# Attention scores in shared columns: 18 steps a segment instead of 20, with a new opening and a new order

## The chip, the cores and the metric

The kernel runs on one core of a Trainium2 chip. The core's engines work side by side, each with its own queue of instructions: the tensor engine (PE, with its weight loads shown as PEld), VectorE (DVE), ScalarE (ACT), GpSimd (POOL) and SyncE (SP), which issues most of the DMA transfers. The metric is the device time of one execution in microseconds (us); the shorter, the better. Before the change the median of three runs is 550.27 us (549.77 to 551.29).

## The reference

Two layers of attention and two of a gated feed-forward block (FFN) alternate over 2048 tokens of width 512. Attention has 32 heads of 16 channels and works on four segments of 512 tokens, one after the other. Inside a segment it is causal softmax attention; beside it each segment reads a memory that earlier segments have summed up.

```python
def _A_ref(x, wq, wk, wv, wo, beta):
    ...
    for s in range(N):                      # N = 4 segments of L = 512
        qs, ks, vs = (q[:, :, s].copy(), k[:, :, s].copy(), v[:, :, s].copy())
        logits = jnp.einsum('bhqd,bhkd->bhqk', qs, ks) * scale + mask
        p = _softmax(logits, axis=-1)
        a_dot = jnp.einsum('bhqk,bhkd->bhqd', p, vs)
        pq = phi(qs)
        a_mem = jnp.einsum('bhld,bhde->bhle', pq, M) / (jnp.einsum('bhld,bhd->bhl', pq, z)[..., None] + 1e-06)
        outs.append(g * a_mem + (1.0 - g) * a_dot)
        pk = phi(ks)
        M = M + jnp.einsum('bhld,bhle->bhde', pk, vs)
        z = z + jnp.einsum('bhld->bhd', pk)
    ...
def _B_ref(x, w_gate, w_up, w_down):
    return _gelu(x @ w_gate) * (x @ w_up) @ w_down
x = x + _A_ref(_layernorm(x), ...)
x = x + _B_ref(_layernorm(x), ...)
x = x + _A_ref(_layernorm(x), ...)
x = x + _B_ref(_layernorm(x), ...)
```

## The kernel before, in words

The work is cut into eight segments `k` (NK): four of the first pair of layers and four of the second. Attention (class `Att`) and FFN (class `Ffn`) of a segment go through the same engines as those of its neighbours, mixed so that PE always has something to issue.

**Scores.** The heads of a segment lie in four blocks `b` of eight; in a block, four even heads (`par` 0) and four odd ones (`par` 1) are worked on together. Keys stand on partitions, queries in columns. A *step* (`steps_of`, L154) fills 512 columns for each of four heads: two PSUM tiles `st` of 128 x 1024. The four heads sit in four groups of 32 rows of the PE array ("row tiles", `tile_position=(32 * j, 0)`, L974): even heads read keys from `kf`, rows 32j to 32j + 16, odd heads from `kB`, a copy of the keys in which the even heads' rows are zero, so that 32 rows can be used. Causality leaves of the 4 key tiles `ki` 512, 384, 256 and 128 columns, 1280 for a head, and two and a half steps hold 1280 columns: five steps a block and parity pair, 20 a segment. ScalarE takes the exponential of each `st` into `pt` (L1005, 128 x 1024), and GpSimd sets the part above the diagonal of a diagonal tile to zero (`affine_select`, L992). `PT_STEPS` = 5 sets of `pt` buffers go round.

**Flushes.** `flush_item` (L1013) multiplies a block's finished `pt` with V (L1039): four pieces, one for each key tile, each as four matmuls side by side in groups of 32 columns of the array ("column tiles"). `vaug` holds, for each head, 16 channels of V and a constant, which gives the softmax's sum. DVE then transposes, divides and transposes back (L1063 to L1078), and POOL adds the memory's part (L1082).

**Everything else on PE** (projections, the memory's products, gate, up, down, the output product) runs through `product` (L524 to L527): four matmuls in column tiles, 512 columns in a group of four.

**Order.** The whole order is written at build time. `Clocks` keeps an estimated time for each engine; work items carry a due time (`DUE`, `DUE_STEP`, `BIAS` and the constants from L42 to L70) and a condition; the loop at L1396 takes the next step of scores when its PSUM is free, else a step of the open item, else a ready item, and, where nothing is ready, a filler product with the tile `warm`. Every engine's queue then has this fixed order, and each instruction waits for the semaphores of what it reads.

**Opening** (L1272 to L1328, outside the planner). 17 filler matmuls run while the first 512 tokens arrive. DVE takes the statistics of four tiles (`bn_stats`, `bn_aggr`), POOL turns them into scales (`first_scale`), DVE normalises (`normed`), PE transposes (`first_turn`), and the first K and Q follow. `gate` (two DVE operations on the memory's gate) stands between the second and the third normalised tile. For segment 0, `kB` of block 0 is made by DVE, that of the other blocks by four DMA copies (`odd_heads`, L692).

**Copies on SP's queue.** Four copies of 64 KB a segment fill `kB`; transposing DMAs turn normalised rows (`xnT`), the memory's output (`amT`) and `phik`; weights and outputs go through the same queue. Three sets of Q, K, `kB` and `vaug` go round (`SETS`).

Of the kernel before, what the change touches and what calls it, by code (L numbers as in the profile page):

```python
# [18 lines left out]
P = 128  # L19
# [17 lines left out]
STEPS = 20  # L37
BY_PE = {("xnTf", 0)}
M_BANKS = 4
PT_STEPS = 5  # L40
SETS = 3
# [3 lines left out]
N3 = 0.0  # L45
GELU_TILES = 2
QK_DUE = 0.696
E_Q = -0.446
E_K = 1.142

FLUSH_WAIT = 5.222
PIECE_SLACK = 3.936
URGENT, SOON, NORMAL = -9.238, -1.856, 0.0
EXP_SLACK, E_SLACK, PHI_SLACK, GELU_SLACK = -0.955, 5.474, 2.934, 5.676
ACT_EVICT, FIRST_EVICT = 4.1, -0.181
XN_BUFS = 4
XN_KEPT = 1
XNA1_PE = 0
NORM_HALVES = 8
RAWS = [7, 7, 9, 6, 8, 8, 10]  # L60
FLUSH_FIRST = -1.999
SECOND_EVICT = 0.375
E_BUFS = 2
KB_SLACK = 8.054
HALF_STEPS = 2
LAST_FIRST = 8
MARGIN = 1.7
PHI_MARGIN = 1.7
KB_MARGIN = 1.5
MEM_SLACK = -2.323  # L70


DUE = {"wo": 0.456, "gate": 1.084, "up": 1.34, "down": 1.726, "upd": 0.124, "mem": 0.239, "v": -0.013}
DUE_STEP = {"gate": 0.0103, "up": 0.0229, "down": 0.0643}
BIAS = {
    **{("qk", *k): d for k, d in {
# [4 lines left out]
    }.items()},  # L81
    **{("mem", *k): d for k, d in {
        (0,): 0.334, (0, 0): -0.435, (1,): -0.094, (1, 0): 0.056, (2,): 0.396, (3,): 0.144, (3, 0): 0.04,
        (4,): -0.223, (4, 0): -0.207, (5,): -0.239, (5, 0): -0.057, (6,): -0.101, (6, 0): 0.015, (7,):
        -0.117, (7, 0): 0.048
    }.items()},
    **{("down", *k): d for k, d in {
# [4 lines left out]
    }.items()},  # L92
    **{("upd", *k): d for k, d in {
        (0,): -0.507, (0, 0): 0.188, (1,): 1.18, (1, 0): 0.412, (2,): -0.142, (2, 0): 0.095, (3,): 1.042,
        (3, 0): -0.249, (4,): -0.368, (4, 0): 0.137, (5,): 0.506, (5, 0): -0.155, (6,): 0.023, (6, 0):
        0.323, (7,): 0.107
    }.items()},
    **{("v", *k): d for k, d in {
# [4 lines left out]
    }.items()},  # L103
    **{("wo", *k): d for k, d in {
# [3 lines left out]
    }.items()},  # L108
    **{("gate", *k): d for k, d in {
# [5 lines left out]
    }.items()},  # L115
    **{("up", *k): d for k, d in {
# [4 lines left out]
    }.items()},  # L121
    **{("num", *k): d for k, d in {
# [5 lines left out]
    }.items()},  # L128
    **{("ek", *k): d for k, d in {
# [14 lines left out]

def bias(kind, k, i=None):
    return BIAS.get((kind, k), 0) + BIAS.get((kind, k, i), 0)


HALF = L // 2
SPLIT = {NK - 1}  # L150
EARLY = 1


def steps_of(k):  # L154


# [76 lines left out]
class Clocks:  # L233
# [57 lines left out]
    def made(self):  # L291

        return self.pe + 0.15
# [1169 lines left out]
```

## Time and profile before

| | |
|---|---|
| median of three runs | 550.27 us (549.77 to 551.29) |
| profiled execution, whole | 550.23 us |
| its span from the first to the last instruction | 548.5 us |
| PE busy | 542.0 us, 99% |
| ScalarE busy | 442.3 us, 81% |
| VectorE busy | 418.5 us, 76% |
| GpSimd busy | 270.9 us, 49% |
| granted PE clock | 1.000 |

In the profile's rows, "L527 PE MATMUL m<-xnT,wu_sb 128*32 128x512" is line 527 on PE, writing tile `m` from `xnT` and `wu_sb`, 128 rows by 32 columns of the array, 512 columns streamed; "x40" counts instructions, and the figures behind the bar are busy time, mean duration of one, and idle time before with what ended it. In a timeline the first two columns are start and length in us. In rows of waits the figures are the total, the count and the longest. In the chain of waits they are start and length along the chain.

### The profile page before, as it was taken

The numbers are of one execution on the slowest core, as the hardware profiler recorded it, in microseconds if no ns is written. First come the engines' busy times: TensorE is split into PE (matmuls) and PEld (weight loads), VectorE is DVE, ScalarE is ACT, GpSimd is POOL, SyncE is SP. The second block draws the span as 40 slices with busy tenths as digits, with TensorE's granted clock in tenths as the row PEclk, the third lists the DMA queues.
The fourth block names the chain that finished last, engine by engine and source line by source line (L and its number), as shares of the span: only waits on it lengthen the run. The fifth ranks groups of instructions, "written<-read, shape, count | busy, mean of one in ns | idle before, by whom it ended". The sixth has DMA issues, their size and how long they took to land.

```text
span 548.5 us, 25412 instructions
## 1 busy us (share of the span) xinstructions
PE 542.0 (99%) x11372; PEld 263.5 (48%) x11372; DVE 418.5 (76%) x790; ACT 442.3 (81%) x530; POOL 270.9 (49%) x541
## 2 busy tenths in 40 slices
PE   8999999999999999999999999999999999999997
PEld 4333444444454444444444444444454445545984
DVE  5878895899869798678777798587985789776162
ACT  5899999997999779987799879998889777872500
POOL 4686553576635664627542466257662472322000
PEclk9999999999999999999999999999999999999999
DMA  7357535140633125200230123111431005102201
GB/s 231 47 125 223 116 42 146 22 51 14 73 56 43 11 41 80 50 13 12 41 60 12 23 31 61 32 20 43 50 72 22 3 12 89 23 3 51 32 5 41
DMA packets 69885, 29.11 MB, mean 53 GB/s; under 512 B 59280, under 2 KB 69264, under 8 KB 69776
## 3 DMA queue, kind: packets, MB, share of 16 engines
q1 hardware_dynamic: 69632, 27.48, 26.1%
q8 instruction: 89, 1.46, 1.2%
q14 instruction: 20, 0.16, 0.1%
q10 hardware_dynamic: 144, 0.01, 0.0%
HBM read 9.71 MB, written 2.10 MB: 22 GB/s over the span
## 4 chain that ended last, share of the span: by engine, by line
PE 89%; DVE 5%; ACT 2%; issue 1%; DMA 1%; POOL 0%; DVEq 0%; ACTq 0%
PE m L527 71%; PE st L974 10%; PE m L1039 6%; ACT pt L1005 2%; DVE x_sb L1137 1%; PE m L425 1%; DVE st L550 1%; DMA xnT<-xn 1%; PE m L887 1%; DVE byq L1063 0%; DVE e L790 0%; DVE phiq L772 0%; DVE xn L586 0%; DVE aT L1078 0%; DVE e L798 0%
## 5 line engine op out<-in xcount | busy, mean ns | idle before, releaser
L1005 ACT ACTIVATE pt<-st 128x1024 bf16<-128x1024 f32 x320 | 309.6, 1029 | 54.6 <-PE st L974 49.7
L992 POOL TENSOR_SCALAR_AFFINE_SELECT pt<-pt 128x512 bf16<-128x512 bf16 (+2 forms) x416 | 197.6, 493 | 189.2 <-ACT pt L1005 182.4
L527 PE MATMUL m<-xnT,wg_sb 128*32 128x512 bf16 (+1 forms) x2016 | 106.2, 356 | 0.4 <-DMA xnT<-xn 0.3
L527 PE MATMUL m<-wd_sb,gel 128*32 128x512 bf16 (+2 forms) x1848 | 106.2, 373 | 0.0
L527 PE MATMUL m<-xnT,wu_sb 128*32 128x512 bf16 (+1 forms) x2016 | 105.7, 356 | 0.0
L1226 DVE TENSOR_TENSOR gel<-gel,m 128x512 bf16<-128x512 bf16 x112 | 75.4, 683 | 37.9 <-PE m L527 35.3
L527 PEld LDWEIGHTS <-wu_sb 128*32 128x32 bf16 x2016 | 51.4, 97 | 39.8 <-issue 5.6
L527 PEld LDWEIGHTS <-wg_sb 128*32 128x32 bf16 x2016 | 51.3, 97 | 38.8 <-issue 5.5
L527 PEld LDWEIGHTS <-gel 128*32 128x32 bf16 x1848 | 46.7, 97 | 45.3 <-issue 6.2
L1063 DVE STREAM_TRANSPOSE byq<-m 128x512 f32<-128x512 f32 x64 | 45.1, 705 | 29.6 <-PE m L1039 29.2
L1137 DVE TENSOR_TENSOR x_sb<-x_sb,m 128x512 bf16<-128x512 bf16 (+1 forms) x65 | 42.0, 662 | 21.7 <-PE m L527 21.7
L1039 PE MATMUL m<-pt,vaug 128*32 128x256 bf16 (+3 forms) x1088 | 46.2, 293 | 0.0
L1191 ACT ACTIVATE gel<-m 128x512 bf16<-128x512 f32 x57 | 32.0, 601 | 16.9 <-PE m L527 16.8
L1082 POOL TENSOR_TENSOR aT<-aT,amT 128x512 bf16<-128x512 bf16 (+1 forms) x28 | 28.5, 1028 | 27.5 <-DMA amT<-am 14.6
L974 PE MATMUL st<-q,kB 32*128 32x256 bf16 (+3 forms) x544 | 41.2, 292 | 0.0
L550 DVE BATCH_NORM_STATS2 st<-x_sb 128x6 f32<-128x512 bf16 x60 | 40.6, 676 | 0.3
L974 PE MATMUL st<-q,kf 16*128 16x256 bf16 (+3 forms) x544 | 40.1, 294 | 0.1
L527 PE MATMUL m<-xnT,wq_sb 128*32 128x512 bf16 x496 | 35.7, 381 | 0.1
L1039 PEld LDWEIGHTS <-vaug 128*32 128x32 bf16 x1088 | 25.3, 97 | 20.8 <-issue 5.3
L527 PE MATMUL m<-xnT,wk_sb 128*32 128x512 bf16 x496 | 34.2, 380 | 0.0
L527 PE MATMUL m<-wv_sb,xnT 128*32 128x512 bf16 x512 | 33.4, 381 | 0.1
L974 PEld LDWEIGHTS <-kf 16*128 16x128 bf16 x544 | 12.4, 91 | 42.8 <-issue 41.5
(94 smaller groups left out, 554.9 us busy)
## 6 DMA issues: line engine op xcount, KB each, us to landing
out_dram<-x_sb SPq DMA_DIRECT2D x15, 128.0 KB, 1.9
wg_sb<-in_B_w_gate_dram SPq DMA_DIRECT2D x8, 224.0 KB, 3.8
kB<-kf SPq DMA_DIRECT2D x28, 64.0 KB, 2.4
wu_sb<-in_B_w_up_dram SPq DMA_DIRECT2D x8, 224.0 KB, 4.4
wd_sb<-in_B_w_down_dram SPq DMA_DIRECT2D x7, 256.0 KB, 4.6
x_sb<-in_A_x_dram SPq DMA_DIRECT2D x3, 512.0 KB, 6.3
xnT<-xn SPq DMA_TRANSPOSE x56, 2.5
x_sb<-in_A_x_dram SPq DMA_DIRECT2D x4, 128.0 KB, 3.0
```

The costliest lines, as they stand in the source:

```text
L425: nc.tensor.matmul(ps[:], lhsT=warm[:], rhs=wide, start=True, stop=True)
L527: nc.tensor.matmul(out[r], lhsT=lhsT[:, r], rhs=rhs, start=start, stop=stop, tile_position=(0, 32 * c))
L550: nc.vector.bn_stats(out=self.st6[:, 0, :], in_=x_sb[:, self.tt0 + j, :])
L974: nc.tensor.matmul(sts[j // 2][:, j % 2, c0:c0 + q1 - q0], lhsT=lhsT[rows, b, P * ki:P * ki + P], rhs=self.q[rows, b, q0:q1], start=True, ...
L992: nc.gpsimd.affine_select(out=dv, in_=dv, pattern=[[0, w], [1, P]], compare_op=ALU.is_ge, fill=0.0, base=0, channel_multiplier=-1)
L1005: 1.024, lambda st=st, tile2=tile2: nc.scalar.activation(out=tile2[:], in_=st[:], func=ACT.Exp, scale=SCALE), told), table="exp")
L1039: nc.tensor.matmul(ps()[32 * j:32 * j + 32, q0 + shift:q1 + shift], lhsT=self.vaug[:, ki, h * (DH + 1):h * (DH + 1) + 32], rhs=step["pt"][ ...
L1063: nc.vector.transpose(out=self.byq[:, c], in_=ps()[:])
L1082: nc.gpsimd.tensor_tensor(out=self.aT[:, b, where], in0=self.aT[:, b, where], in1=self.amT[b][:, where], op=ALU.add)
L1137: ck.dve.post(ck.made(), slack, (0.15 + 0.533 * n / D, lambda: nc.vector.tensor_tensor(out=xt, in0=xt, in1=ps()[:, 0:n], op=ALU.add), lamb ...
L1191: return lambda: nc.scalar.activation(out=out(), in_=in_(), func=ACT.Gelu_apprx_tanh)
L1226: ck.dve.post(ck.made(), NORMAL, (0.683, lambda: nc.vector.tensor_tensor(out=hidden(g, h), in0=hidden(g, h), in1=banked(ps), op=ALU.mult), ...
```

## The change

**Steps.** In segments 1 to 6 blocks (0, 1) and (2, 3) form pairs, in segment 0 blocks 1 and 2; segment 7 stays as it was. In a paired block, the first 64 queries of each diagonal tile see only the tile's first 64 keys. For these 64 x 64 pieces, even and odd heads share the same columns: even heads write PSUM partitions 0 to 63, odd heads 64 to 127 (`BOTH`). One step holds them all for two blocks (2 blocks x 4 key tiles x 64 columns). What is left of a head is 448, 320, 192 and 64 columns, 1024 in all, two steps. A pair thus takes nine steps instead of ten. `RINGS` gives ordinary steps five sets of `pt` and shared steps one.

**Shared columns in PE.** A shared step issues, for each of its 8 pieces and 4 row groups, a matmul from `kf` at `tile_position=(32 * j, 0)` and one from `kB` at `(32 * j, 64)`: 64 matmuls of 64 columns.

**Flushes and V.** A paired flush has eight pieces instead of four: four of its own parity and four of 64 columns from the shared step. The latter use `vpair`, in which V of the first 64 keys of each tile stands on partitions 0 to 63 for even heads and on 64 to 127 for odd heads, zeros elsewhere. For this, V's columns are sorted by parity (all even heads first), and two DMA copies a segment fill `vpair`, after V's four evictions and after the last flush of the segment before. `vpair` has one buffer.

**Masks.** A shared step is masked by two selects over 1024 elements for each half; the other diagonal pieces are 64 columns wide.

**Sets.** Q and `kB` have two sets, K and V three; the copies into `kB` wait for the scores of the segment two before.

**Opening.** Tile 2's mean and variance are taken by ScalarE (`Copy` and `Square` with sums), DVE has one product for them, and `gate` goes to the planner's queue for 14 us. `kB` of segment 0 is made by DVE in all four blocks. The columns of constants of `vaug` 1 and 2 move from ScalarE to POOL. The planner's clocks start 0.7 us earlier (`SHIFT`).

**Order.** `DUE`, `DUE_STEP`, `BIAS` and the scalar constants have new values, so that the whole order is another. The `RUSH` branches have no effect at `RUSH = 0`.

```diff
+Q = P // 2
+BOTH = 2
+PAIRED = {k: [(0, 1), (2, 3)] for k in range(NK - 1)} | {0: [(1, 2)]}
-PT_STEPS = 5
-SETS = 3
+RINGS = 5, 1
+SETS_Q, SETS_K, SETS_V, SETS_B = 2, 3, 3, 2
...
+            first = b == pairs[b][0]
+            for par in range(2):
+                shared = first and par == 0
+                found += [([(b, par, 3, 3 * P + Q, L, 0), (b, par, 0, Q, L, Q)], []),
+                          ([(b, par, 1, P + Q, L, 0), (b, par, 2, 2 * P + Q, L, L - P - Q)],
+                           [] if shared else [(b, par, None)])]
+                if shared:
+                    found.append(([(c, BOTH, ki, P * ki, P * ki + Q, 4 * Q * (c - b) + Q * ki)
+                                   for c in pairs[b] for ki in range(TPS)], [(b, 0, None)]))
...
-                    if par:
-                        lhsT, rows = self.kB, slice(32 * j, 32 * j + 32)
-                    else:
-                        lhsT, rows = self.kf, slice(32 * j, 32 * j + 16)
-                    nc.tensor.matmul(sts[j // 2][:, j % 2, c0:c0 + q1 - q0], lhsT=lhsT[rows, b, P * ki:P * ki + P],
-                                     rhs=self.q[rows, b, q0:q1], start=True, stop=True, tile_position=(32 * j, 0))
+                    rhs = self.q[32 * j:32 * j + 32, b, q0:q1]
+                    out = sts[j // 2][:, j % 2, c0:c0 + q1 - q0]
+                    if par in (0, BOTH):
+                        m = P if par == 0 else Q
+                        nc.tensor.matmul(out[0:m], lhsT=self.kf[32 * j:32 * j + 16, b, P * ki:P * ki + m], rhs=rhs[0:16],
+                                         start=True, stop=True, tile_position=(32 * j, 0))
+                    if par in (1, BOTH):
+                        m = 0 if par == 1 else Q
+                        nc.tensor.matmul(out[m:P], lhsT=self.kB[32 * j:32 * j + 32, b, P * ki:P * ki + P - m], rhs=rhs,
+                                         start=True, stop=True, tile_position=(32 * j, m))
...
+                if r:
+                    where = [(small[0:Q], 16, Q, 0), (small, 16, Q, Q)]
+                elif inner == [0, Q]:
+                    where = [(blocks[:, :, 0, :].rearrange("p j (a c) -> p j a c", c=Q), 4, Q, Q)]
+                elif inner:
+                    where = [(tile2[:, :, c0:c0 + Q], 2, Q, Q) for c0 in inner]
...
+                todo = ([(par, 0, 0), (par, 3, 0), (par, 1, 0), (par, 2, 0)] + [(BOTH, ki, 0) for ki in range(TPS)] if paired else
+                        [(par, ki, 0) for ki in ((0, 1, 3, 2) if par == 0 else (0, 2, 1, 3))])
...
-                              and ck.has(*[("v", k, j) for j in rows])
+                              and ck.has(*[("v", k, j) for j in rows], *([("vpair", k)] if paired else []))
...
+                    if self.n_v == TPS and k not in HALVED:
+                        ck.when(lambda: "vpair0" in ev and (k == 0 or ("flush", k - 1, 3, 1) in ev), lambda: shifted(max(t, ck.pe)))
+                def shifted(t):
+                    half = VW // 2
+                    for rows, cols in ((slice(0, Q), slice(0, half)), (slice(Q, P), slice(half, VW))):
+                        ck.sp.post(t, KB_SLACK, (0.55, lambda rows=rows, cols=cols: nc.sync.dma_start(
+                            out=vpair[rows, :, cols], in_=self.vaug[0:Q, :, cols]),
+                            lambda t2: ck.at(t2 + 1.8, lambda: there(t2 + 2.0))))
...
+    nc.scalar.activation(out=junk[:], in_=x_sb[:, 2, :], func=ACT.Copy, scale=-1.0 / D, accum_out=sums[:, :, 0])
+    nc.scalar.activation(out=junk[:], in_=x_sb[:, 2, :], func=ACT.Square, bias=sums[:, 0, 0:1], accum_out=sums[:, :, 1])
+    nc.scalar.activation(out=sums_column(0)[0], in_=sums_column(0)[1], func=ACT.Copy)
     first_stats(0)
     first_stats(1)
     first_aggr(0)
     first_aggr(1)
     first_scale(0)
-    first_stats(2)
-    first_aggr(2)
     first_stats(3)
     first_aggr(3)
+    nc.vector.tensor_tensor(out=n0.mv[:, 2:3, :], in0=sums[:], in1=parts[:], op=ALU.mult)
     first_scale(1)
     a0 = att[0]
-    a0.made()
-    n0.first_rows = [n0.normed(j, j) for j in range(2)]
-    gate()
-    n0.first_rows += [n0.normed(j, j) for j in range(2, TPS)]
+    a0.made[0](), a0.made[1]()
+    n0.first_rows = [n0.normed(j, j) for j in range(TPS)]
...
-    streams = [(k, t) for k in range(NK) for t in range(STEPS)]
+    counts = [len(steps_of(k)) for k in range(NK)]
+    streams = [(k, t) for k in range(NK) for t in range(counts[k])]
```

More of the change, by code (lines that the diff above doesn't have):

```diff
@@ L477, in scale @@
                     [32, 4, 2, DH]), op=ALU.mult)
-        for i in range(1, SETS):
+        ck.dve.post(14.0, NORMAL, (0.6, gate, None))
+        ck.pool.post(12.0, MEM_SLACK, (1.9, lambda: nc.gpsimd.memset(vpair[:], 0.0), lambda t: ev.update({"vpair0": t})))
+        for i in range(1, SETS_B):
             ck.pool.post(14.0 * i, MEM_SLACK, (1.9, lambda i=i: nc.gpsimd.memset(kBs[i][:], 0.0), None))
@@ L482, in later_constants @@
             ck.pool.post(24.0 + 4.0 * i, MEM_SLACK, (0.5, lambda i=i: nc.gpsimd.memset(mblks[i][:], 0.0), None))
+        for i in range(1, SETS_V):
+            ck.pool.post(16.0 + 3.0 * i, MEM_SLACK, (0.5, lambda i=i: nc.gpsimd.tensor_copy(
+                out=sums_column(i)[0], in_=sums_column(i)[1]), None))
         for c in range(4):
@@ L688, in odd_heads @@
             def odd_heads(t):
[L690 removed]
+                b0 = 0 if k else KB_DVE
                 self.n_kf += 1
@@ L753, in phi_done @@
         @staticmethod
-        def phi_done(k):
-            s = k % NSEG
-            return all((s == 0 or ("phiq", k, b) in ev) and (s == NSEG - 1 or ("phik", k, b) in ev) for b in range(4))
+        def phi_done(k, name, none):
+            return k % NSEG == none or all((name, k, b) in ev for b in range(4))
         def phi_q(self, half, ready, slack):
@@ L1107, in done @@
                 ck.dve.post(ck.made(), soon, *steps)
-            cost = sum(pc[8] - pc[7] for pc in pieces) / 2400.0 + 0.02
-            last_k = 7 if k - 1 in SPLIT else 3
+            cost = sum(max(pc[9] - pc[8], 85) for pc in pieces) / 2400.0 + 0.02
+            last_k = 7 if k - 1 in HALVED else 3
             before = ("back", k, chunk - 2) if chunk > 1 else ("back", k - 1, last_k - 1 + chunk) if k else None
@@ L1350, in next_e @@
     def next_e():
-        now = streams[0][0] + streams[0][1] / STEPS if streams else 1e9
+        now = streams[0][0] + streams[0][1] / counts[streams[0][0]] if streams else 1e9
         act = ck.act
@@ L1398 @@
         next_e()
-        halves = score_now()
+        halves = () if rushed() else score_now()
         if halves:
@@ L1412 @@
             late = ck.pe - (FLUSH_FIRST if ("scores", 0) not in ev else FLUSH_WAIT)
-            got = next((it for it in items if (it.kind != "flush" or not streams or it.posted < late
-                                               or len(steps_made) - PT_STEPS >= len(steps_done)) and it.ready()), None)
+            got = next((it for it in items if it.kind in ("wo", "turn") and it.k < RUSH and it.ready()), None)
+            got = got or next((it for it in items if (it.kind != "flush" or not streams or it.posted < late
+                                               or any(len(steps_made[r]) - RINGS[r] >= len(steps_done[r]) for r in range(2))) and it.ready()), None)
             if got:
```

245 lines of the change are left out of this document (142 added, 103 removed), and 77 rows, old and new, of the table BIAS.

## The prediction

> **What bounds the kernel now.** I read the page's header and engine rows first, then the slices, then what the tensor engine waited for, then the chain of waits, and last the tensor engine's timeline in the middle of the run.
>
> ```profile
> span 548.5 us, 25412 instructions
> PE 542.0 (99%) x11372; PEld 263.5 (48%) x11372; DVE 418.5 (76%) x790; ACT 442.3 (81%) x530; POOL 270.9 (49%) x541
> ...
> PEclk9999999999999999999999999999999999999999
> ...
> PE 89%; DVE 5%; ACT 2%; issue 1%; DMA 1%; POOL 0%; DVEq 0%; ACTq 0%
> ```
> ```profile
> PE m L425 <- DVE warm L416: 1.1, 1, 1.1
> PE m L887 <- issue: 0.6, 1, 0.6
> PE m L939 <- DVE xnT L629: 0.3, 1, 0.3
> PE m L527 <- DMA xnT<-xn: 0.3, 1, 0.3
> ```
> PE is busy for 99% at a full clock, and all its waits together are 2.3 us. A busy PE could still be a PE that is fed filler, so the filler group matters:
>
> ```profile
> L425 PE MATMUL m<-warm 128*128 128x512 bf16 x20 | 7.8, 556 | 1.1 <-DVE warm L416 1.1
> L527 PE MATMUL m<-warm 128*32 128x512 bf16 x32 | 2.3, 379 | 0.0
> ```
> After the opening only 32 matmuls, 8 groups of four, are filler. So PE's own stream of work is the bound nearly from end to end, and this change is priced by what it takes out of that stream. ScalarE is different:
>
> ```profile
> L1005 ACT ACTIVATE pt<-st 128x1024 bf16<-128x1024 f32 x320 | 309.6, 1029 | 54.6 <-PE st L974 49.7 <-POOL pt L992 3.0 <-POOL ve L567 1.1
> ```
> It waited 49.7 us for scores. The change makes 294 of these exponentials instead of 320, and 26 x 1.029 = 26.8 us less of ScalarE looks like the prize; but an engine that waits for PE returns nothing directly when it gets shorter. At most it removes part of PE's 2.3 us of waits, and I book nothing for it.
>
> What a step of scores costs PE is read from starts, since the ends are modelled:
>
> ```profile
> 299.89 2.34 PE L527 MATMUL m<-xnT,wu_sb 128*32 128x512 bf16 x40
> 302.17 0.40 PE L974 MATMUL st<-q,kB 32*128 32x512 bf16 x4
> 302.49 1.26 PE L527 MATMUL m<-xnT,wu_sb 128*32 128x512 bf16 x20
> 303.58 0.72 PE L1039 MATMUL m<-pt,vaug 128*32 128x512 bf16 x16
> 304.13 0.82 PE L527 MATMUL m<-xnT,wu_sb 128*32 128x512 bf16 x12
> 304.88 0.40 PE L974 MATMUL st<-q,kB 32*128 32x384 bf16 x8
> 305.21 0.61 PE L527 MATMUL m<-xnT,wu_sb 128*32 128x512 bf16 x8
> ```
> ```profile
> 288.61 8.20 PE m L527 x152
> ```
> The last row, from the chain, gives the unit: 152 / 4 = 38 groups of four in 8.20 us, 0.216 us a group of 512 columns. From 299.89 to 302.49 there are ten groups (2.16) and one step: the step takes 0.44. From 304.13 to 305.21 there are three groups (0.65) and one step: 0.43. I use 0.43. Of it 0.22 is the step's 512 columns; the other 0.21 is the passage from column tiles to row tiles and back. Half of a removed step is therefore switching.
>
> **The change part by part.** *Steps.* I counted the order in which the two programs issue matmuls. Before, PE goes to row tiles 185 times (160 steps, some sent in two halves). After, 147 steps (19 in the first segment, 18 in six, 20 in the last) take 161 visits: 147 ordinary and 14 with shared columns (12 whole, two halves). Ordinary visits: 185 x 0.43 = 79.6 us before, 147 x 0.43 = 63.2 after. That is 16.4 us less.
>
> *Shared steps.* A shared step is 64 matmuls of 64 columns into 64 partitions, a tile that no row of the trace has. Its switching is 0.21. For its body the nearest rows are bursts of tiny matmuls:
>
> ```profile
> 307.72 0.44 PE L527 MATMUL m<-zcols,phiq 128*32 128x8 bf16 x40
> 308.00 0.41 PE L527 MATMUL m<-wd_sb,gel 128*32 128x512 bf16 x4
> ```
> ```profile
> 404.01 0.70 PE L887 MATMUL m<-vaug,phik 128*32 128x32 bf16 x64
> 404.53 0.41 PE L527 MATMUL m<-xnT,wg_sb 128*32 128x512 bf16 x4
> ```
> 40 of them pass in 0.28 us (7.0 ns each) and 64 in 0.52 (8.1 ns each), weight loads included. So 64 cost 0.45 to 0.52 if the issue limits. The stream asks 8 pieces x 64 columns for two parities: 0.22 us if all eight tiles stream at once, 0.43 if the two tiles of one row group take turns. I take 0.50. Bounds: 0.22 below (all at once, no issue limit); above, nothing overlaps within a row group, from the weight loads:
>
> ```profile
> L974 PEld LDWEIGHTS <-kB 32*128 32x128 bf16 x544 | 12.9, 92 | 27.1 <-issue 26.9
> ```
> Half of 92 ns for half the columns is 46, plus 27 of stream, 16 times in each row group: 1.17 us. Fourteen visits at 0.50 + 0.21 add 9.9 us (6.0 to 19.3).
>
> The bursts above already bear on this bound: in 404.01 each column tile uses all rows, and 64 pairs of load and matmul need 0.52 us on four tiles, 32 ns a pair on each, far below one load's 92 ns; loads and streams of the same rows do overlap there.
>
> The Trainium skill, page "TensorE: Matmul & The Clock Gate", section "The mechanism", says that a weight load overlaps running matmuls only where its row group differs, which speaks against this change, since both parities of a shared step sit in one row group. With that page's load time of columns / 1.2, by estimate 53 ns, a body would be 16 x (53 + 27) = 1.28 us and the sum below would end at about 6 us slower than now. The burst's 32 ns disagrees with the rule for column tiles; no run here has the 64-column tile.
>
> *Flushes.* The 52 flushes of paired blocks go from 1280 columns in four pieces to 448 + 320 + 192 and five pieces of 64. Before, 303.58 to 304.13 shows 0.55 (1280 / 512 x 0.216 = 0.54). After: 960 / 512 x 0.216 = 0.405, plus five groups of 64 columns. The 32-column burst gives 0.033 a group, and 64 columns stream in 0.027, so 0.033 each and 0.57 in all: +0.03 x 52 = +1.6 us. Bounds: at 0.028 (the 8-column burst) +0.2; at 0.054, what 128 columns stream in, +7.0. I take the burst, whose size is nearest. The 64-column piece in 52 ordinary steps adds 0.006 each, +0.3.
>
> *Filler.* Ten groups for eight: +0.4.
>
> *The copies.* Each paired segment needs a second V (vpair), two copies on SP's queue behind the four evictions of V and the previous segment's last flush; every later issue on that queue (transposes of xn and am, weights) stands behind them. The nearest copy:
>
> ```profile
> kB<-kf SPq DMA_DIRECT2D x28, 64.0 KB, 2.4
> ```
> Cover: V is projected well ahead, and its first reader comes late. By the changed program's order and the durations above, 6.7 to 9.6 us of PE work lie between a shared step and the first flush that reads it. Booked at 0; an uncovered copy would be 2.4 us once a segment, 7 x 2.4 = 16.8 us at the very most.
>
> *Masks.* A shared step is masked by two selects of 1024 elements for each half:
>
> ```profile
> L992 POOL TENSOR_SCALAR_AFFINE_SELECT pt<-pt 128x1024 bf16<-128x1024 bf16 x8 | 8.6, 1091 | 4.5 <-ACT pt L1005 4.5
> ```
> From scores to the last mask: one exponential 1.03 and four selects 4.36, 5.4 us, against at least 6.7 of cover. Booked at 0, with 1.3 us to spare. The queue behind is POOL's own: later masks and adds to aT, for which flushes and output products wait. In total POOL is little changed (some 60 large selects replace small ones) and only 49% busy. A single buffer set for shared steps makes ScalarE wait for the pair's last flush before the next shared exponential; other exponentials queue behind it, while ScalarE has 49.7 us of such waits already.
>
> *The beginning.* One tile's statistics move from VectorE to ScalarE, the gate's two operations leave this stretch:
>
> ```profile
> 6.21 0.18 DVE L1282 BATCH_NORM_AGGREGATE mv<-st 128x2 f32<-128x6 f32 x1
> 6.31 0.66 DVE L1279 BATCH_NORM_STATS2 st<-x_sb 128x6 f32<-128x512 bf16 x1
> ...
> 7.28 0.29 POOL L1285 TENSOR_SCALAR ve<-mv 128x2 f32<-128x2 f32 x1 [0.56 <-DVE mv L1282]
> ...
> 7.65 0.77 POOL L1287 TENSOR_TENSOR rs<-ve,mhalf 128x2 f32<-128x2 f32 x1
> ...
> 8.46 0.73 DVE L586 TENSOR_SCALAR xn<-x_sb,mv,rs 128x512 bf16<-128x512 bf16 x2
> ...
> 10.62 0.61 PE L939 MATMUL m<-xnT,wq_sb 128*128 128x256 bf16 x4 [0.30 <-DVE xnT L629]
> ```
> Without 0.66 + 0.18 of statistics the second pair's scale ends some 0.6 earlier, and PE's wait at 10.62 with it: -0.6 (0 if ScalarE is late, -0.84 at most).
>
> *Sum:* -16.4 + 9.9 + 1.6 + 0.3 + 0.4 - 0.6 = -4.8 us. The profiled execution took 550.23 us for its span of 548.5 (1.7 around it); the median of the runs shown is 550.27, the same. 550.2 - 4.8 = 545.4 us.
>
> **The rivals.**
> 1. *The shared tile runs better than a burst.* For it: eight tiles instead of four, so each load has longer. Body 0.30: 14 x 0.20 = 2.8 less, 542.6 us. Against: the issue rate of the bursts.
> 2. *A new wait takes the gain.* Place: the first flush after a shared step, whose mask ends 1.3 us before it is needed. For it: ScalarE's order also holds Gelu blocks of about 1 us, and one ahead of the exponential uses up the spare. Against: PE waited just 2.3 us so far. It cancels the forecast at 4.8 / 13 = 0.37 us a shared step: about 550.
> 3. *Slower: loads and streams of one row group do not overlap in the 64-column tile.* Place: each shared step; price 1.17 instead of 0.50, 14 x 0.67 = +9.4: 554.8 us. It decides from a body of 0.50 + 4.8 / 14 = 0.84 us on. Against it the burst's 32 ns a pair.
> 4. *It does less than it says.* Excluded for the count: the orders show 147 steps for 160.
>
> **How the numbers follow.** Forecast 0.54, rival 1 0.16, rival 2 0.20, rival 3 0.10. About 0.3%, 1.65 us, is what a measurement can tell from no change: below 548.6 is faster, above 551.9 slower. Faster: 0.54 + 0.16 + 0.03 of rival 2 = 0.73. Same: 0.11 of rival 2. Slower: 0.06 of it and rival 3, 0.16. The range goes from 541.5 (body at its lower bound, 14 x 0.28 = 3.9 less) to 549.5 (4.1 more, part of dearer flush pieces or of waits); it leaves out rival 3, the upper half of rival 2 and little below.
>
> **What would show it.** In the changed kernel's timeline: a shared step of 0.65 to 0.75 us from its start to the next product; a paired flush of 0.57; ordinary steps still 0.43; PE's waits still under 4 us; first scores at about 11.2 us instead of 11.8; ScalarE about 27 us less busy with a longer wait for scores. I am wrong if PE shows idle time ahead of flushes that read vpair (rival 2), or if the shared steps take over 1 us (rival 3).

## The result and the profile after

The changed kernel takes 552.37 us (median of 20 executions, 550.76 to 558.03) against 549.75 us before (548.98 to 551.29): a ratio of 1.0061, 95% interval 1.0045 to 1.0077. It is slower by about 3 us, where 5 us less were forecast. Taken again beside other kernels it is 1.0038 (1.0014 to 1.0061), so slower in both, by 0.4 to 0.6%. Four of its 20 executions took 557 to 558 us, at a granted clock of 0.993 to 0.997; the other 16 took 550.8 to 554.1. The profiled execution took 551.75 us for its span of 550.0.

The page of the changed kernel, the lines that answer to those of before (header, engines, instruction fetches with count, MB and share, the exponentials):

```profile
span 550.0 us, 28751 instructions
PE 537.4 (98%) x13044; PEld 277.9 (51%) x13044; DVE 425.8 (77%) x799; ACT 417.4 (76%) x501; POOL 270.8 (49%) x536
...
q8 instruction: 102, 1.67, 1.3%
...
L1084 ACT ACTIVATE pt<-st 128x1024 bf16<-128x1024 f32 x294 | 285.3, 1029 | 71.6 <-PE st L1044 47.6
```

PE is busy for 4.6 us less, and the span is longer by 1.5. ScalarE is 24.9 us less busy, and its idle time ahead of the exponentials grew from 54.6 to 71.6 us: it gave nothing back. So PE now waits. Its waits in the changed kernel (total, count, longest):

```profile
PE m L660 <- DVE xn L620: 1.9, 2, 1.2
PE m L561 <- issue: 1.6, 2, 1.3
PE m L561 <- DVE gel L1310: 1.1, 1, 1.1
PE m L447 <- DVE warm L438: 1.1, 1, 1.1
PE st L1040 <- ACT pt L1084: 0.8, 2, 0.6
PE m L1122 <- DMA vpair<-vaug: 0.6, 1, 0.6
PE m L561 <- DVE macc L979: 0.5, 1, 0.5
PE m L561 <- DVE am L904: 0.3, 1, 0.3
PE m L561 <- DMA wd_sb<-in_B_w_down_dram: 0.2, 1, 0.2
PE m L561 <- DVE macc L983: 0.2, 1, 0.2
```

The list of before held four waits, 2.3 us. This one holds ten, 8.3 us, with VectorE, ScalarE, transfers and issue behind them, and no single wait over 1.3 us. The list leaves out short waits and those that hide in modelled ends, so I also counted from the starts of all PE instructions: where two starts lie further apart than they otherwise do for that kind, the excess over 0.06 us is a wait. Split in this way, the spans are (us):

| | before | after | the best kernel below (e10_both) |
|---|---|---|---|
| first scores start | 11.8 | 12.3 | 11.3 |
| PE's waits after that | 2.7 | 9.6 | 6.1 |
| the rest, PE's own work | 534.0 | 528.1 | 527.4 |
| span | 548.5 | 550.0 | 544.8 |

The work fell by 5.9 us, more than the sum forecast. The waits took 6.9 and the opening 0.5. Of the 6.9, 2.3 more are waits for VectorE, 2.7 more for the issue of the instruction itself, 0.7 for transfers, 0.6 each for ScalarE and for the rest.

*The work.* The changed kernel's timeline of PE, a shared step and a paired flush (start, length, both in us):

```profile
300.81 0.60 PE L561 MATMUL m<-xnT,wu_sb 128*32 128x512 bf16 x8
301.35 0.21 PE L1040 MATMUL st<-q,kf 16*64 16x64 bf16 x1
...
301.85 0.21 PE L1044 MATMUL st<-q,kB 32*64 32x64 bf16 x1
301.99 1.05 PE L561 MATMUL m<-xnT,wu_sb 128*32 128x512 bf16 x16
```
```profile
113.92 0.62 PE L1122 MATMUL m<-pt,vaug 128*32 128x448 bf16 x16
114.36 0.30 PE L1122 MATMUL m<-pt,vpair 128*32 128x64 bf16 x16
114.47 0.40 PE L561 MATMUL m<-wd_sb,gel 128*32 128x512 bf16 x4
```

The 64 matmuls of the shared step start within 0.50 us, and from the first to the next product are 0.64. Two groups before it take 2 x 0.216, so 0.11 goes into entering: 0.75 in all here, 0.74 in the median of the 12 whole ones. The flush takes 0.55 (113.92 to 114.47), as a whole flush did before.

*The opening.* All engines of the changed kernel, from 7 us:

```profile
7.02 0.73 POOL L1371 TENSOR_TENSOR rs<-ve,mhalf 128x2 f32<-128x2 f32 x1
...
7.71 1.96 POOL L509 MEMSET vpair<- 128x2236 bf16 x1
7.78 2.34 DVE L620 TENSOR_SCALAR xn<-x_sb,mv,rs 128x512 bf16<-128x512 bf16 x2 [0.29 <-POOL rs L1371]
...
9.87 0.71 PE L660 MATMUL m<-ident,xn 128*128 128x128 bf16 x8 [1.17 <-DVE xn L620]
...
12.29 0.39 PE L1040 MATMUL st<-q,kf 16*128 16x512 bf16 x4
```

The scale `rs` comes earlier, as forecast: VectorE begins the second pair at 7.78 instead of 8.46. But the pair takes 2.34 us instead of 0.73, beside a memset of `vpair` that POOL has begun 0.07 us sooner. The Trainium skill, page "SBUF — State Buffer", section "Who interferes with whom", says that GpSimd and some VectorE operations take turns at a shared pair of ports, that the one that issues first keeps it for its whole instruction, and that the other stands still. The rows agree, as far as the rough spans of POOL can say: the pair takes 1.61 us longer than before, most of the memset's 1.96, and ends at 10.12, 0.45 us after the memset.

*VectorE behind masks.* The same thing in the middle; all engines of the changed kernel:

```profile
97.93 4.66 POOL L1071 TENSOR_SCALAR_AFFINE_SELECT pt<-pt 64x1024 bf16<-64x1024 bf16 x4 [0.43 <-ACT pt L1084]
...
100.38 1.15 DVE L860 TENSOR_SCALAR e<-e 128x512 bf16<-128x512 bf16 x1
...
101.56 1.56 DVE L852 SCALAR_TENSOR_TENSOR e<-kf,e 128x512 bf16<-128x512 bf16 x1
...
103.05 0.68 DVE L1310 TENSOR_TENSOR gel<-gel,m 128x512 bf16<-128x512 bf16 x1
...
103.78 0.59 PE L561 MATMUL m<-xnT,wu_sb 128*32 128x512 bf16 x5 [1.13 <-DVE gel L1310]
```

Four selects of a shared step hold POOL from 97.93 to 102.59. VectorE's two operations on `e`, begun in that time, take 2.71 us instead of 0.98 (0.28 and 0.69 in the median of before; the rows are under e3). The product of gate and up (`gel`) comes after them, its PSUM tile comes free late, and PE stands 1.1 us.

*Transfers.* The changed kernel's SP queue and PE, around the second segment's copies into `vpair`:

```profile
59.00 3.77 SPq L406 DMA_DIRECT2D wu_sb<-in_B_w_up_dram  x6
62.86 1.37 SPq L793 DMA_DIRECT2D vpair<-vaug  x2
...
68.84 0.30 PE L1122 MATMUL m<-pt,vpair 128*32 128x64 bf16 x16 [0.63 <-DMA vpair<-vaug]
```

The copies are issued right behind six loads of weights and land 5.9 us later, where the median of the 14 copies is 2.8. Later the last five loads of `wd_sb` are issued at 106.00, behind transposes on the same queue that wait for VectorE; before, all seven were issued from 83.41 on.

*Issue.* The longest wait of the changed kernel has neither a semaphore nor a transfer of data behind it (PE's timeline, then the fetches of the page of before):

```profile
397.33 0.65 PE L561 MATMUL m<-zcols,phiq 128*32 128x8 bf16 x60
399.28 0.19 PE L561 MATMUL m<-zcols,phiq 128*32 128x8 bf16 x4 [1.30 <-issue]
```
```profile
q8 instruction: 89, 1.46, 1.2%
```

It stands inside a burst of 64 tiny matmuls, 60 of which have gone. The stream of instructions has become longer (13044 matmuls for 11372, each with its weight load) and is fetched in 102 pieces instead of 89, 16 KB each (1.67 MB / 102). Whether the fetch causes the wait is left to the experiments.

### The profile page after: what moved, and what is told of

Its sections match the earlier page's. It is cut to its first block, busy times and chain, and to the rows that moved or that the text cites. A ratio compares the mean times of both kernels' runs of the same rounds, so it can differ in the third digit from the quotient of the medians.

```text
span 550.0 us, 28751 instructions
## 1 busy us (share of the span) xinstructions
PE 537.4 (98%) x13044; PEld 277.9 (51%) x13044; DVE 425.8 (77%) x799; ACT 417.4 (76%) x501; POOL 270.8 (49%) x536
## 3 DMA queue, kind: packets, MB, share of 16 engines
q8 instruction: 102, 1.67, 1.3%
## 4 chain that ended last, share of the span: by engine, by line
PE 85%; ACT 4%; DVE 3%; DMA 3%; issue 2%; POOL 1%; SPq 0%; ACTq 0%; DVEq 0%; POOLq 0%
PE m L561 68%; PE m L1122 6%; PE st L1040 5%; PE st L1044 4%; ACT gel L1275 2%; ACT pt L1084 2%; DMA vpair<-vaug 1%; DVE gel L1310 1%; DMA wd_sb<-in_B_w_down_dram 1%; DMA amT<-am 1%; POOL pt L1071 1%; DMA x_sb<-in_A_x_dram 1%; PE m L949 1%; ACT L1084 0%; DVE e L860 0%
## 5 line engine op out<-in xcount | busy, mean ns | idle before, releaser
L1084 ACT ACTIVATE pt<-st 128x1024 bf16<-128x1024 f32 x294 | 285.3, 1029 | 71.6 <-PE st L1044 47.6
L1071 POOL TENSOR_SCALAR_AFFINE_SELECT pt<-pt 128x128 bf16<-128x128 bf16 (+3 forms) x416 | 199.3, 499 | 182.8 <-ACT pt L1084 177.9
L561 PE MATMUL m<-xnT,wg_sb 128*32 128x512 bf16 (+1 forms) x2016 | 108.5, 356 | 0.5 <-DVE am L904 0.3
L561 PEld LDWEIGHTS <-gel 128*32 128x32 bf16 x1848 | 50.3, 97 | 39.2 <-issue 5.3
L1040 PE MATMUL st<-q,kf 16*128 16x64 bf16 (+4 forms) x960 | 41.0, 241 | 0.8 <-ACT pt L1084 0.8
L1122 PE MATMUL m<-pt,vaug 128*32 128x64 bf16 (+6 forms) x1088 | 41.0, 272 | 0.1
L1044 PE MATMUL st<-q,kB 32*64 32x64 bf16 (+3 forms) x960 | 39.1, 241 | 0.0
L1040 PEld LDWEIGHTS <-kf 16*128 16x128 bf16 (+1 forms) x960 | 17.6, 97 | 37.7 <-issue 36.4
L561 PE MATMUL m<-xnT,wq_sb 128*32 128x512 bf16 x496 | 33.3, 380 | 0.0
L552 DVE CAST gel<-m 128x512 bf16<-128x512 f32 x43 | 29.0, 681 | 5.4 <-PE m L561 5.0
```

The costliest lines, as they stand in the source:

```text
L561: nc.tensor.matmul(out[r], lhsT=lhsT[:, r], rhs=rhs, start=start, stop=stop, tile_position=(0, 32 * c))
L1040: nc.tensor.matmul(out[0:m], lhsT=self.kf[32 * j:32 * j + 16, b, P * ki:P * ki + m], rhs=rhs[0:16], start=True, stop=True, tile_position=( ...
L1044: nc.tensor.matmul(out[m:P], lhsT=self.kB[32 * j:32 * j + 32, b, P * ki:P * ki + P - m], rhs=rhs, start=True, stop=True, tile_position=(32 ...
L1071: nc.gpsimd.affine_select(out=dv, in_=dv, pattern=[[0, n] for n in dv.shape[1:-1]] + [[1, c]], compare_op=ALU.is_ge, fill=0.0, base=base, ...
L1084: 1.024, lambda st=st, tile2=tile2: nc.scalar.activation(out=tile2[:], in_=st[:], func=ACT.Exp, scale=SCALE), told), table="exp")
L1122: nc.tensor.matmul(ps()[32 * j:32 * j + 32, q0 + shift:q1 + shift], lhsT=va[:, ki, h * (DH + 1):h * (DH + 1) + 32], rhs=step["pt"][j // 2] ...
```

## The experiments

All ratios are to the kernel before on the same chip, with 95% intervals. e1 is the base of e3 to e8, e10 and e11.

**e1_memset_early**: `vpair` is cleared while POOL is idle.

```diff
     for va in vaugs:
         nc.gpsimd.memset(va[:, :, VW:], 0.0)
+    nc.gpsimd.memset(vpair[:], 0.0)
...
-        ck.pool.post(12.0, MEM_SLACK, (1.9, lambda: nc.gpsimd.memset(vpair[:], 0.0), lambda t: ev.update({"vpair0": t})))
+        ck.pool.post(12.0, MEM_SLACK, (1.9, None, lambda t: ev.update({"vpair0": t})))
```

> The kernel after, with the memset of vpair moved into GpSimd's idle time near 2.7 us; every other instruction keeps its place. Theory (VectorE is blocked while GpSimd runs one long instruction): the third and fourth normalised rows, 2.03 us for the first of them in the profile after, take 0.37 each, PE's wait of 1.33 us near 9.9 us goes, the first scores start at 11.2 us instead of 12.3, and the kernel gains about 1 us (ratio to before 1.004). Rival (the rows were late for another reason, such as the scale from GpSimd): the first scores stay at 12.3 us and the ratio at 1.006.

Measured: 549.34 us, 0.9997 (0.9981 to 1.0013); first scores at 10.48 us. Its opening, all engines:

```profile
2.63 1.96 POOL L487 MEMSET vpair<- 128x2236 bf16 x1
...
7.43 0.74 DVE L621 TENSOR_SCALAR xn<-x_sb,mv,rs 128x512 bf16<-128x512 bf16 x2 [0.31 <-POOL rs L1372]
```

With nothing else moved, the pair takes 0.74 again, first scores come 1.8 us sooner, and the loss to before is gone: 0.4 to 0.6% against the two results of the changed kernel, 2 to 3.5 us. The profile shows only 1.0 us of this (span 549.0), but its execution took 550.76, above the median. Nor are the 1.8 us of the opening all the memset's: VectorE's first pair already begins 0.4 us earlier here (6.38 against 6.76), and with the same early memset e3, e5 and e10 show their first scores at 11.2 to 11.3, where the filler matmuls ahead of the first transposes end later (17 of them take 6.64 us in e3, 5.75 in e1). So the opening gains 1.0 to 1.8 us.

**e2_memset_in_before**: the reverse, in the kernel before. One of its memsets (`kB`, 1.80 us) goes to the same place.

```diff
-            ck.pool.post(14.0 * i, MEM_SLACK, (1.9, lambda i=i: nc.gpsimd.memset(kBs[i][:], 0.0), None))
+            ck.pool.post(14.0 * i, MEM_SLACK, (1.9, (lambda i=i: nc.gpsimd.memset(kBs[i][:], 0.0)) if i > 1 else None, None))
...
     first_scale(1)
+    nc.gpsimd.memset(kBs[1][:], 0.0)
```

> The kernel before, with its memset of the second kB (1.8 us on GpSimd) moved from near 14 us to right behind the two scales of the opening, where the kernel after has that of vpair. Theory of blocking: the third row takes about 1.9 us instead of 0.37, the first scores start at 13.0 us or later instead of 11.8, and the time grows by 1 to 1.5 us (ratio 1.002 to 1.003). Rival: nothing changes (11.8 us, ratio 1.000).

Measured: 550.63 us, 1.0021 (1.0009 to 1.0032); first scores at 13.16 for 11.81. All engines:

```profile
8.38 1.80 POOL L1299 MEMSET kB<- 128x2048 bf16 x1
8.46 2.18 DVE L586 TENSOR_SCALAR xn<-x_sb,mv,rs 128x512 bf16<-128x512 bf16 x2 [0.22 <-POOL rs L1287]
...
10.39 0.40 PE L626 MATMUL m<-ident,xn 128*128 128x128 bf16 x4 [1.34 <-DVE xn L586]
```

The place of one memset costs the kernel before about 1.1 us (0.5 to 1.8 by the interval), by the same two rows. This cause is shown from both sides.

**e3_no_select**: e1 without the selects of the shared steps.

```diff
                 def mask(dv, w, c, base):
+                    if r:
+                        return
```

> The kernel with the early memset, and the 52 selects of the shared steps left out (the part above the diagonal of the shared columns stays unmasked); the order of all else is kept. Theory (selects of 1.1 us block VectorE, which then is late for PE): VectorE's longest doubled operations (1.5 us for 0.69 in e<-kf, 1.1 for 0.28 in e<-e) disappear in segments 1 to 6, PE's wait of 1.3 us near 104 us goes, and 2 to 3 us are gained against the early memset alone (ratio 0.999 to 1.000). Rival (the waits belong to the new order, not to the selects): under 1 us is gained.

Measured: 548.02 us, 0.9975 (0.9960 to 0.9990), 1.2 us better than e1 by the ratios. VectorE's operations on `e` in the second segment (60 to 120 us), ns min/median/max, first of the kernel before, then of the changed kernel, then of e3:

```profile
L798 DVE TENSOR_SCALAR e<-e x7: 278/284/396, 65.3 to 117.3; 128x512 bf16<-128x512 bf16 x7
L790 DVE SCALAR_TENSOR_TENSOR e<-kf,e x7: 691/694/853, 65.6 to 117.6; 128x512 bf16<-128x512 bf16 x7
```
```profile
L860 DVE TENSOR_SCALAR e<-e x6: 269/308/1148, 70.5 to 113.6; 128x512 bf16<-128x512 bf16 x6
L852 DVE SCALAR_TENSOR_TENSOR e<-kf,e x6: 692/1224/1564, 70.9 to 113.9; 128x512 bf16<-128x512 bf16 x6
```
```profile
L861 DVE TENSOR_SCALAR e<-e x6: 278/290/487, 69.7 to 111.4; 128x512 bf16<-128x512 bf16 x6
L853 DVE SCALAR_TENSOR_TENSOR e<-kf,e x6: 691/809/1529, 70.0 to 111.9; 128x512 bf16<-128x512 bf16 x6
```

The selects stretch VectorE's work, and PE's wait for `gel` at 103.8 is gone without them. Not every long operation goes: the two of 1.53 us that are left in this stretch of e3 stand beside another operation of POOL, the addition to `aT`. The gain lies between what the two theories said, and the intervals of e1 and e3 overlap: the mechanism is shown, its price only as "about 1 us". PE still waits 8.2 us, so the masks are not most of it.

**e4_unpaired**: e1 with 20 steps in each segment, in the new order's constants.

```diff
-PAIRED = {k: [(0, 1), (2, 3)] for k in range(NK - 1)} | {0: [(1, 2)]}
+PAIRED = {k: [] for k in range(NK)}
```

> The kernel with the early memset and no paired blocks: 20 steps in every segment, planned with the new constants. Work on PE: 5 to 6 us more than the kernel after. If PE's waits come with the shared steps (selects, vpair, single buffer set), they fall from 11 us to some 4 and the ratio is about 1.000; if they come with the new constants and the order they make, they stay near 10 and the ratio is 1.012 or more.

Measured: 557.11 us, 1.0137 (1.0121 to 1.0152). It doesn't price the pairing alone, since the planner now finds nothing ready far more often. The filler group of e4, which has 40 matmuls (10 groups) in the changed kernel:

```profile
L562 PE MATMUL m<-warm 128*32 128x512 bf16 x160 | 12.2, 384 | 0.0
```

40 filler groups for 10: 30 x 0.216 = 6.5 us of the 7.7 us to e1. The expectation's two branches do not separate: the waits fall to 3.7 us, as the first has it, and the ratio is that of the second. The waits are fewer without the shared steps, their masks, copies and flushes; but 30 groups of filler may stand where waits would have been, so this run alone does not say what the waits came with.

**e5_dma_order**: e1 with four of the six loads of `wu_sb` that stand ahead of the second segment's `vpair` copies sent behind them, and the loads of `wd_sb` in two batches, four and three, at their first two places.

```diff
+    def piece_of(i):
+        if wu0 + 3 <= i < wu0 + 7:
+            return lambda: None
+        if i >= wd0:
+            return lambda: [send(n) for n in range(wd0, wd0 + (4 if i == wd0 else 7))]
...
                             out=vpair[rows, :, cols], in_=self.vaug[0:Q, :, cols]),
+                            k == 1 and rows.start and [send(n) for n in range(wu0 + 3, wu0 + 7)]),
```

> The early memset, and on SP's queue two changes of order in the first 120 us: four loads of wu_sb go behind segment 1's two copies of vpair instead of ahead of them, and the seven loads of wd_sb go out with the first two of them instead of behind transposes that wait for VectorE. All else keeps its place. Theory (copies and loads come late because of what stands ahead of them on SP's queue): PE's wait for vpair near 67 us (1.2 us with the early memset) and that for wd_sb near 113 us (0.3 to 1.6) both go, and 1 to 2.5 us are gained against the early memset (ratio 0.995 to 0.998). Rival (PE then waits at the next late operand instead): under 0.5 us is gained.

Measured: 548.58 us, 0.9984 (0.9972 to 0.9996), 0.7 us better than e1 and less than expected. Both waits are gone (in the trace the flush's `vpair` pieces follow at once, 66.59, 67.03, and the next product at 67.14), but PE's waits after the first scores fall by only 2.0, from 10.6 to 8.6: others grew, such as one for `am`, 0.9 us.

**e6_split_selects**: e5 with each shared select cut into two of 512 elements, so that VectorE can get between.

```diff
+                    if r and w == 16:
+                        mask(dv[:, 0:8], 8, c, base)
+                        mask(dv[:, 8:16], 8, c, base)
+                        return
```

> The kernel with the DMA order above, and each select of a shared step in two of 512 elements (0.63 us each instead of 1.14 for the whole), nothing left out. Theory (it is the length of one GpSimd instruction that VectorE is blocked for): VectorE's longest doubled operations fall from 1.5 to about 1.1 us, PE's wait of 1.3 us near 102 us shrinks to under 0.8, and 0.3 to 1 us is gained against the DMA order. Rival (the sum of GpSimd's time counts, which grows by some 7 us): the time stays or grows by up to 1 us.

Measured: 548.26 us, 0.9981 (0.9970 to 0.9992), no different from e5. The wait at 102 us went, others of 0.4 and 0.5 came. The halves take 0.67 us each, so POOL's time on these selects grows; VectorE's longest operation on `e` in the second segment is still one of 1.53, beside the addition to `aT`, as in e3. A gain of 0.3 to 1 us was expected and none can be told from the noise.

**e7_shifted_stream**: e1 with 32 matmuls of 64 columns instead of four fillers of 512 in the opening. The work before the first tile is about as long; everything behind stands 28 matmuls, with their weight loads 56 instructions, later in the stream.

```diff
-    keep_warm(WARM, 0)
+    keep_warm(WARM - 4, 0)
+    ps = bank_tile(0, [P, L])
+    for _ in range(32):
+        nc.tensor.matmul(ps[:, 0:Q], lhsT=warm[:], rhs=warm[:, 0:Q], start=True, stop=True)
```

> The early memset, and in the opening 32 tiny matmuls in place of four filler ones, which moves all later PE instructions by 56 places in the stream (28 matmuls with their weight loads). Theory (the waits marked issue come from the fetch of PE's instructions in pieces of fixed size): the wait of 1.4 us near 400 us, at the same matmul in each profile so far, moves or goes, and other issue waits appear elsewhere; in sum within 1 us of the early memset. Rival (something in the program holds PE there): it stays at the same matmul with 1.3 to 1.5 us.

Measured: 547.28 us, 0.9965 (0.9948 to 0.9983), 1.8 us better than e1 by the ratios, though 28 matmuls longer (the intervals overlap by a little). PE's timeline of e7 at the same burst:

```profile
394.09 0.41 PE L565 MATMUL m<-zcols,phiq 128*32 128x8 bf16 x32
394.98 0.37 PE L565 MATMUL m<-zcols,phiq 128*32 128x8 bf16 x32 [0.48 <-issue]
```

In the changed kernel, e1, e3, e5, e6 and e9 the burst stops for 1.2 to 1.8 us with 60 of its matmuls gone; here it stops after 32, 28 earlier, for 0.6. The stop keeps its place in the stream of instructions and not in the work. That fits a fetch in fixed pieces. The 1.8 us are not its price, though: in the lists of PE's waits those for issue go from 1.2 us in e1 to 0.5 in e7, but those for transfers (`vpair` and `wd_sb`) from 2.5 to 0.4. Why the transfers are in time here is open.

**e8_booked_cost**: e1, where the planner books 0.53 us instead of 0.32 for a shared step, nearer to the measured one.

```diff
-            ck.on_pe(0.32 if r else 0.23)
+            ck.on_pe(0.53 if r else 0.23)
```

> The early memset, with the planner booking 0.53 us for a shared step instead of 0.32, so that the whole order is planned anew; the profile after showed 0.50 to the last matmul and 0.64 to the next product. If the later waits come from this one wrong price, PE's waits fall from 9.6 us to under 6 and the ratio to 0.995 or less. If the order is good because its constants were fitted to just this plan, another plan has more fillers and waits, and the ratio is 1.003 or more.

Measured: 552.74 us, 1.0060 (1.0046 to 1.0075); waits of 10.7 us and three more filler groups. A truer price makes another order, and a worse one, as the second branch said; that the other constants belong to the old price is the likely reason, and not tested further.

**e9_after_again**: the changed kernel unchanged, beside e10 and e11.

> The kernel after, unchanged, on the same chip as the next two. Ratio to before 1.004 to 1.008, as measured first; in its profile the third normalised row again takes about 2 us, and PE's waits from 12 us on are again 8 to 11 us.

Measured: 551.16 us, 1.0038 (1.0014 to 1.0061), just below the range expected. Its profile has the same second pair in the opening (2.34 us for 0.73) and the same stop in the burst, so these are the kernel's and not one execution's.

**e10_both**: e1, e5 and the shift of e7 together. **e11_shifted_twice**: e5 with 72 tiny matmuls for 9 fillers, 126 instructions later.

```diff
-    keep_warm(WARM - 4, 0)
+    keep_warm(WARM - 9, 0)
...
-    for _ in range(32):
+    for _ in range(72):
```

> The early memset, the DMA order on SP's queue and the stream shifted by 56 instructions together. Theory (the kernel's loss is made of separate waits, each with its own cause, on a body of PE work that is 6 us shorter): first scores at 10.5 to 11.3 us, no wait for vpair or wd_sb, the issue wait near 395 us under 0.7, ratio 0.993 to 0.997. Rival (what one change frees is lost at the next wait): no better than the shifted stream alone, 0.9965, or worse.

> As the kernel with all three, but shifted by 126 instructions instead of 56. If the issue waits hang on where a burst of short matmuls falls in the fetched pieces, the long one near 395 us changes again (to another length or another matmul) and the time differs from the other shift by up to 1.5 us, either way. If the shift by 56 won for another reason (the opening), both have the same waits and the same time within 0.2%.

Measured: e10 546.55 us, 0.9946 (0.9934 to 0.9958), faster than both kernels (but its interval overlaps that of e7, 0.9948 to 0.9983); e11 548.00 us, 0.9977 (0.9967 to 0.9987). They differ only in the shift. PE's waits of e10, then the first of e11:

```profile
PE m L565 <- DVE gel L1315: 1.1, 1, 1.1
PE m L447 <- DVE warm L438: 1.1, 1, 1.1
PE m L565 <- DVE gel L556: 0.9, 1, 0.9
PE st L1045 <- ACT pt L1089: 0.8, 2, 0.6
PE m L565 <- DVE macc L988: 0.2, 1, 0.2
```
```profile
PE st L1049 <- ACT pt L1089: 1.8, 2, 1.1
...
PE st L1049 <- issue: 0.9, 2, 0.7
PE m L565 <- issue: 0.9, 1, 0.9
```

In e10's list no transfer and no issue is left; counted from starts, waits for issue between work are 0.9 us there and 3.0 in e11. In e11 the burst runs through, and PE stops at other places. The two rows for `pt` make up 2.6 us in e11 and 0.8 in e10, so the stops are not all that the shift changed.

The thirteen traces say more of these stops. There is a fetched piece for every 128 matmuls with their weight loads (11372 / 89 and 13044 / 102). Count the matmuls that stand ahead of a stop, from the program's first one: all 21 stops that are marked issue, come after the opening and exceed the usual distance of their kind by over 0.2 us have 86 to 94 left over after division by 128 (94 early in the run, 86 late, as if a few other instructions lay in the stream). The number is 1502 in the kernel before, 9432 in the changed kernel and in e1, e3, e5, e6, e8 and e9, 9432 again in e7 and e10, where this is 28 matmuls earlier in the work, and 9560, one piece later, in e11. Each of the 21 ends 1.2 to 1.7 us after the transfer of a piece has ended (at 397.87 for the stop that ends at 399.28), and it is always the transfer with the same place in the count: the 73rd for 9432, the 74th for 9560, the 11th for 1502. So PE stops where one piece ends and goes on soon after a transfer. That this transfer brings the piece that PE then starts on is the likely reading; the trace does not name its contents. Not each end of a piece is a stop: e4 has none over 0.2 us. Why some are is argued only: at 7.8 ns a pair 128 tiny matmuls pass in 1.0 us, while one transfer alone takes 0.9 to 2.1 us.

## Why the prediction was wrong

*What bounds the kernel, and ScalarE:* right. ScalarE's 24.9 us came back nowhere.

*The steps and shared steps:* right. An ordinary visit to row tiles takes 0.43 us in the median of both kernels, and the 14 with shared columns take 10.0 us together, where 9.9 were taken. The body is the 0.50 us taken; rival 3 (1.17) falls, and with it the Trainium skill's rule in "TensorE: Matmul & The Clock Gate", "The mechanism", for this tile: two tiles of one row group load and stream beside each other (the 16 pairs of load and matmul of a row group in 0.50 us).

*The flushes:* the term of 1.6 us measured 0: a paired flush takes 0.55 us in the median, as a whole one did before. Its 16 matmuls of 64 columns pass in 0.11 us, 0.028 a group of four, the lower bound of the prediction, where the burst's 0.033 was taken. Without this term the sum is -16.4 + 10.0 + 0.3 + 0.4 = -5.7, and PE's work fell by 5.9 us; the prediction's sum without the opening is -4.2.

*The beginning:* failed in its sign, -0.6 against +0.5. The step priced what was taken out of the stretch and not what came in: a memset on POOL that holds VectorE. It had a planned time of 12 us, but a queue knows only an order, and POOL had nothing to do before it. Without it the first scores come at 10.5 (e1) to 11.3 us (e10), where 11.2 was forecast: what was taken out had been priced about right. e1, e2 and e9 show this.

*Copies and masks, both booked at 0:* failed. Flushes hardly waited for masks, at the place that rival 2 named (waits for POOL are under 0.5 us in all); but the same selects stretch VectorE's work, whose buffers PE then lacks. Of the 14 copies one pair lay behind a burst of weight loads and kept PE waiting 0.6 us. What should have been asked of "some 60 large selects" is which engine stands still while they run, and of the two copies what is issued ahead of them, in every segment and not for the median.

*"PE's waits still under 4 us":* this is the step at which the prediction fell: its sum was one of PE's work, with the waits of before carried over unchanged into a new order. They went from 2.7 to 9.6 us. Rival 2 was nearest in time (about 550), yet not in mechanism: no single wait takes the gain, some ten do.

Shown by experiment: the memset, in both directions (about 1.1 us in the kernel before; 2 to 3.5 us by the ratios in the changed one, of which its opening accounts for 1.0 to 1.8); that the selects stretch VectorE's work, and that the late copies and loads lay behind what is issued ahead of them (the waits go with their cause, but the prices, about 1.2 and 0.7 us, lie within the intervals); that PE's long stops in bursts stand where a fetched piece ends (the shifts, and the 21 places). Not shown: that it is the fetch itself that PE waits for, and what these stops cost. Counted from starts they make up 2.5 of the changed kernel's 9.6 us of waits and 0.8 of the 2.7 before; the times of e7 against e1 and of e10 against e11 (1.7 to 1.8 us by the ratios) hold other waits too. Open: what the pairing is worth in an order made for it and for the old one alike, since e4 and e8 both change the filler, and the rest of e10's 6.1 us of waits, the largest part of them for VectorE.

With three repairs that touch no step of scores, e10 gains 3.0 us on the kernel before beside it, of the 4.8 forecast. That its 546.55 us lie only 1.2 above the forecast is in part luck: in its profile PE's own work is 6.6 us less than before, where the sum had 4.2, and its waits are still 3.4 us more, where the sum had none.

## What to carry to other kernels

A kernel whose bound engine is 99% busy under a hand-fitted order owes its few waits to that order, as e4 and e8 suggest; when a change makes the order anew, the waits are a term of the sum, and a few us of saved work can be smaller than it. Of each instruction that a change puts on a helper engine, a memset too, ask what it blocks while it runs, and place it by what stands ahead of it in its queue, not by its planned time. Where a bound engine stops in a burst of tiny instructions with no semaphore behind it, count the matmuls ahead of the stop and compare with the size of a fetched piece, and shift the stream by some tens of instructions, before explaining the time with anything else.

## What the runs showed of the hardware

Column tiles of 64 over row groups of 16 or 32 rows take a weight load and a matmul in 7.8 ns (64 in 0.50 us), as the tiny bursts before did (7.0 to 8.1).

A memset, a select or an addition of POOL that has begun first holds some of VectorE's operations beside it for most of its length: two scales took 2.34 us instead of 0.73 beside a memset of 1.96 us, and 2.18 beside one of 1.80; a 0.28-us operation on `e` took 1.15 beside selects of 1.14 us, and one of 0.69 took 1.53 beside an addition to `aT`. Others run on: three products `gel` beside the same selects (from 97.98) took 0.67 to 0.68 us each, the usual 0.68.

PE's instructions are fetched in pieces of 16 KB, one for every 128 matmuls with their weight loads. In 12 of 13 profiles PE stops for 0.25 to 1.8 us where a piece ends, at the same matmul in every run with the same stream (1.2 to 1.8 us in a burst of 64 in six profiles), and goes on 1.2 to 1.7 us after a piece's transfer; with a shift of 28 matmuls the stop stood 28 matmuls earlier in the work, and with one of 63 it left the burst. With nothing but these two shifts between them, two kernels differ by 0.3% (0.9946 and 0.9977).
